# A planned attention and gate kernel: V made once per chunk and copied by DMA, a joint rsqrt chain, half the out transposes, output summed in DRAM

## The chip, the cores and the metric

One core of a Trainium2 chip runs the whole program. The metric is the device time of one execution in microseconds (us); of several executions the median is taken.

## The reference

```python
xn = _layernorm(x)                       # x: 1 x 2048 x 512, bf16
q = (xn @ wq)  -> 32 heads of 16         # wq: 512 x 512
k = xn @ wk ; v = xn @ wv                # one k and one v of 16 columns for all heads
p = softmax(q k^T * 16**-0.5)            # 32 heads x 2048 x 2048
s = concat_heads(p @ v) @ wo             # wo: 512 x 512
g = silu(silu(xn @ w1) @ w2)             # w1: 512 x 1792, w2: 1792 x 512
out = x + s * g
```

## The kernel before

The 2048 rows are 16 tiles of 128, in 4 chunks of 512 queries. A group g is one chunk of queries and four heads (half e of the eight-head block oi = g // 2); there are 32 groups. Each group has 64 slots: 32 blocks of 64 keys, times two head pairs i. One slot is one score unit: four matmuls 64x32 by 512 into one PSUM bank, and then an exponential of that bank (128x512). So there are 2048 units, 1240 of which ACT exponentiates and 808 DVE.

A unit's exponential is made in one of two ways:

- **On ACT**: an ACTIVATE Exp from PSUM into `pa_sb` (L1674), for one bank or for two banks at once.
- **On DVE**: one TENSOR_SCALAR from PSUM that writes the bits of a rough exponential into `db_sb` (L1042). Eight such slots make a batch. Three more copies of the batch with shifted bits are then made in `ds_sb`, by GpSimd's INT64_ADD on 64-bit words (one for each copy, L1225) or, near the end, by DVE (L1221). The four versions enter the sum with weights `SHIFT_W`.

The products with V (`do_pv`, L1303) go to one PSUM bank per group; V carries a column of weights so that the softmax's sum comes with it. `make_norm` then transposes the bank (L1320), takes a reciprocal (L1323), multiplies (L1325), and for each pair of groups transposes 128x512 into `on_sb` (L1335), from which the out projection reads. The MLP runs as jobs `h` and `z` (L705), the query projection as job `q`, the out projection as job `w` (L705, and L1514 and L591 for the last chunk).

TensorE is used as two lanes (rows and columns split, tiles of 64x32), fed from one queue: scores on lane 1, V products on lane 0, the halves of jobs on either.

**What sets the order.** The program is written by a planner (class `Planner`) that steps the five engines with a table of durations and latencies, picks the next piece for each, and writes down five instruction queues with the semaphore waits that they need. Each engine runs its queue in order. `Mix.draw` shakes the planner's thresholds once per stretch by the numbers in `SEEDS`, so the order is that of one drawn plan.

**The prologue.** Per chunk: BN_STATS of four tiles (L539), a chain of eight tiny DVE instructions for the inverse square root (L556 to L565, the tiles in sets `first`), the scaled tiles `xn_sb` (L568), transposes on TensorE (L607) and their copies `xnT_sb` (L618), then the jobs K (L633, copied by DVE in L651) and V. Job V (L670) makes each 64-key block twice, into PSUM rows 0 to 63 and 64 to 127:

```python
for r in (0, 64):
    h = pe.matmul(bank(b)[r:r + 64, t * DH:(t + 1) * DH],
                  lhsT=xnT_sb[:, dc, kb * 64:(kb + 1) * 64], rhs=wv_sb[:, dc, :],
                  start=(dc == 0), stop=(dc == NDC - 1), tile_position=(0, r), skip_group_check=True)
```

DVE then writes five weighted copies straight into `v_sb` (L679). GpSimd fills the weight columns of `v_sb` (L495), zeroes (L501, L497), and sends a shifted copy of the keys by DMA (L1349).

**The end of a row tile.** `final` makes two DVE passes of 128x512, the product with the gate (L814) and the sum with a reloaded x (`xr_sb`, L817), and stores `ob_sb` from SP (L809). The last four tiles take the path of the `tail` functions.

Of the kernel before, what the change touches and what calls it, by code (L numbers as in the profile page):

```python
# [22 lines left out]
SEEDS, STRETCH = [0, 0, 882634, 0, 348373, 328499, 78780, 554384, 89101, 903077, 320169, 0, 878569, 280070, 102111, 381856, 427096, 265022, 0, 740569, 0, 0, 0, 191854, 393933, 374197, 266972, 0, 665170, 0, 882882, 218695, 9227, 955074, 159633, 731624, 518155, 138034, 620799, 357599, 376984, 365473, 457970, 796664, 668429, 641664, 991272, 0, 0, 23990, 593814, 88565, 504692, 394759, 276845, 267858, 882770, 104810, 721623, 135503, 603776, 0, 337714, 100793, 638616, 0, 419715, 752789, 751312, 664693, 308960, 0, 762547, 276261, 218757, 897693, 0, 624478, 290921, 0, 713781, 335568, 417921, 100939, 814701, 0, 180062, 99721, 614963, 258262, 411291, 131548, 802432, 314922, 883804, 569039, 54637, 401726, 110613, 0, 983842, 914345, 0, 0, 0, 0, 0, 0, 0, 0], 6000.0  # L23
STG = lambda j, xn, ev: xn[4 * j - 1].op is not None
# [3 lines left out]
T_P64, DV_MIN, T_LIB = 1868.0, 40, 300.0  # L28
# [5 lines left out]
J_SLIP = 1.014  # L34
NEXT_OB, OB_SLACK = 8, 67.243
NORM_PRIO, T_DIV = 0, 264.0
A_OPEN = 1
T_MS, V_AT = 500.0, 9
T_TP, T_COLD, N_COLD = 56.0, 427.0, 11
# [16 lines left out]
NPA, NDB, NDS, NTM = 27, 3, 4, 4  # L56
MARGIN, MARGIN_END = 17, 20
# [5 lines left out]
ROOM = 1  # L63
# [4 lines left out]
MATE = 176.663  # L68
RH, EVR, SC_PRIO, PES = 0, (0, 2, 3), 0, (1, 0)
# [6 lines left out]
class Task:  # L76
    __slots__ = ("eng", "dur", "emit", "reads", "writes", "prio", "preds", "op", "on_place", "dma", "gate", "ports", "after", "ring", "first")

    def __init__(self, eng, dur, emit, reads=(), writes=(), prio=5, preds=(), on_place=None, dma=0, gate=None, ports=1):
        self.ports, self.after, self.ring = ports, None, None  # L80
# [9 lines left out]
    (DV, PE): 140.0, (DV, AC): 150.0, (DV, DV): 115.0, (DV, PO): 165.0, (DV, SP): 180.0,  # L90
# [5 lines left out]
class Planner:  # L96

    def __init__(self):
# [7 lines left out]
        self.held = None  # L106
# [3 lines left out]
        self.last2 = {DV: None, PO: None}  # L110

# [28 lines left out]
    def place(self, eng, dur, emit, reads, writes, dma=0, t0=None, ports=1, after=None):  # L140
# [23 lines left out]
        elif dma:  # L164
            start = max(t0 + 1400.0, self.dma_t if dma > 1 else 0.0)
# [14 lines left out]
    def tensor(self, mode, lane, dur, emit, reads, writes, t, after=None, n=8, held=None):  # L180
# [18 lines left out]
        if both or lane == 1:  # L199
            self.held = held  # L200
# [18 lines left out]
    def avail(self, task):  # L219
# [35 lines left out]
    def finalize(self, new_sem):  # L255
# [40 lines left out]
        for e in ENGINES:  # L296
            n = 0
            for op in self.order[e]:
# [53 lines left out]
def bass_recurrent_scan__grouped_kv_mqa__dense_activation_silu__prompt_kernel(  # L352
# [29 lines left out]
    with ExitStack() as es:  # L382
# [15 lines left out]
        v_sb = sb("v_sb", [P, K + 1, NKB, 2 * DH], BF16)  # L398
# [43 lines left out]
        xv = xf.rearrange("(t p) d -> p t d", p=P)  # L442

# [53 lines left out]
        pl.add(Task(PO, 1800.0, lambda g: g.memset(kt_sb[0:DH, 1, :], 0.0), [("xn", 3)], [("kt1", c) for c in range(NC)], 3,  # L497
                    gate=lambda: all(xn_task[t].op is not None for t in range(4)), ports=2))
# [36 lines left out]
        for j in range(4):  # L535
            for t in range(4 * j, 4 * j + 4):
                if t == 1:
# [3 lines left out]
                                  gate=(lambda j=j: STG(j, xn_task, evac_kt)) if j > 1 else  # L541
# [4 lines left out]
        first = (2, 2, 4, 4, 4)  # L546
# [75 lines left out]

        def xnT_keys(c):
            return [("xnT", t) for t in range(4 * c, 4 * c + 4)]

        def mk_K(c, ka, kb, bk=None):
# [13 lines left out]
            def consume(jb, op):  # L640
# [18 lines left out]
            job("K", c, 0.0, [(rnd(dc), ["wke"] + keys, max(64.0, n / 2.4 + 3.0)) for dc in range(NDC)], consume,  # L659
                bk=bk, gate=lambda: all(k in pl.lastw for k in keys))  # L660
# [1122 lines left out]
```

## Time and profile before

| | before |
|---|---|
| median of 3 runs | 658.52 us (658.26 to 658.54) |
| profiled execution, its span | 656.6 us (its own time is not given beside it; 1.9 us lie between the span and the median) |
| TensorE busy | 648.1 us (99%) |
| VectorE (DVE) busy | 639.3 us (97%) |
| ScalarE (ACT) busy | 640.4 us (98%) |
| GpSimd (POOL) busy | 571.0 us (87%) |
| granted TensorE clock | 1.00 in every stretch |
| HBM | 8.95 MB read, 2.10 MB written |

Busy is the union of an engine's records. A record of ACT or DVE begins before the one ahead of it has ended, so the sum of durations is above the busy time, and the step from one start to the next is what one instruction costs its engine when work is waiting. Matmuls overlap likewise, and a busy TensorE need not be a full one.

### The profile page before, as it was taken

The numbers are of one execution on the slowest core, as the hardware profiler recorded it, in microseconds if no ns is written. First come the engines' busy times: TensorE is split into PE (matmuls) and PEld (weight loads), VectorE is DVE, ScalarE is ACT, GpSimd is POOL, SyncE is SP. The second block draws the span as 40 slices with busy tenths as digits, with TensorE's granted clock in tenths as the row PEclk, the third lists the DMA queues.
The fourth block names the chain that finished last, engine by engine and source line by source line (L and its number), as shares of the span: only waits on it lengthen the run. The fifth ranks groups of instructions, "written<-read, shape, count | busy, mean of one in ns | idle before, by whom it ended". The sixth has DMA issues, their size and how long they took to land.

```text
span 656.6 us, 44475 instructions
## 1 busy us (share of the span) xinstructions
PE 648.1 (99%) x22180; PEld 330.7 (50%) x19436; DVE 639.3 (97%) x1170; ACT 640.4 (98%) x1128; POOL 571.0 (87%) x320
## 2 busy tenths in 40 slices
PE   8999999999999999999999999999999999999997
PEld 4445554544455554554555454444555555554444
DVE  8999999999999999999999999999999999999976
ACT  6889999999999999999999999999999999999995
POOL 4038899999998978999999878999999999889991
PEclk9999999999999999999999999999999999999999
DMA  6311111000011100000000010000000000100001
GB/s 177 129 48 42 42 28 29 10 4 10 5 35 28 35 28 4 10 4 6 9 4 12 20 36 26 4 5 9 5 10 4 10 21 20 35 11 5 4 4 34
DMA packets 13641, 15.92 MB, mean 24 GB/s; under 512 B 2320, under 2 KB 12816, under 8 KB 13456
## 3 DMA queue, kind: packets, MB, share of 16 engines
q1 hardware_dynamic: 12976, 12.36, 6.3%
q8 instruction: 162, 2.65, 1.7%
q0 software_dynamic: 192, 0.46, 0.2%
q10 hardware_dynamic: 288, 0.26, 0.1%
q14 instruction: 23, 0.19, 0.1%
HBM read 8.95 MB, written 2.10 MB: 17 GB/s over the span
## 4 chain that ended last, share of the span: by engine, by line
PE 84%; ACT 10%; DVE 3%; POOL 1%; DMA 0%; issue 0%
PE ps L967 28%; PE ps L1303 23%; PE ps L705 20%; PE ps L961 13%; ACT pa_sb L1674 9%; ACT t_sb L761 1%; DVE stats_sb L539 1%; DVE xn_sb L568 1%; PE ps L1514 1%; DVE xnT_sb L618 0%; DMA kt_sb<-kt_sb 0%; POOL qt_sb L501 0%; POOL kt_sb L497 0%; DVE v_sb L679 0%; DVE kt_sb L651 0%
## 5 line engine op out<-in xcount | busy, mean ns | idle before, releaser
L1674 ACT ACTIVATE pa_sb<-ps 128x512 bf16<-128x512 f32 (+1 forms) x1038 | 611.0, 771 | 4.1 <-PE ps L967 3.8
L1225 POOL INT64_ADD ds_sb<-db_sb x300 | 562.1, 1896 | 41.5 <-DVE db_sb L1042 31.9
L1042 DVE TENSOR_SCALAR db_sb<-ps 128x512 uint16<-128x512 f32 x808 | 499.9, 680 | 4.2 <-PE ps L961 2.0
L967 PE MATMUL ps<-qt_sb,kt_sb 64*32 64x512 bf16 x5448 | 470.6, 378 | 1.5 <-DVE v_sb L679 0.8
L1303 PE MATMUL ps<-ds_sb,v_sb 64*32 64x512 bf16 x4848 | 350.5, 377 | 0.0
L1303 PE MATMUL ps<-pa_sb,v_sb 64*32 64x512 bf16 x2480 | 269.9, 377 | 0.5 <-DVE v_sb L679 0.5
L961 PE MATMUL ps<-qt_sb,kt_sb 64*32 64x512 bf16 x2744 | 263.6, 375 | 0.0
L967 PEld LDWEIGHTS ps<-qt_sb,kt_sb 64*32 64x32 bf16 x5448 | 130.4, 89 | 162.8 <-ACT pa_sb L1674 70.6
L1303 PE MATMUL ps<-db_sb,v_sb 64*32 64x512 bf16 x1616 | 210.6, 377 | 0.0
L1303 PEld LDWEIGHTS ps<-ds_sb,v_sb 64*32 64x32 bf16 x4848 | 133.4, 91 | 43.5 <-issue 15.0
L705 PE MATMUL ps<-xnT_sb,w_sb 64*32 64x512 bf16 x1792 | 134.6, 377 | 0.0
L705 PE MATMUL ps<-w_sb,u_sb 64*32 64x512 bf16 x1792 | 133.5, 376 | 0.0
L1303 PEld LDWEIGHTS ps<-pa_sb,v_sb 64*32 64x32 bf16 x2480 | 91.4, 91 | 26.8 <-issue 7.9
L1303 PEld LDWEIGHTS ps<-db_sb,v_sb 64*32 64x32 bf16 x1616 | 66.5, 91 | 15.7 <-issue 5.3
L705 PEld LDWEIGHTS ps<-xnT_sb,w_sb 64*32 64x32 bf16 x1792 | 42.8, 91 | 24.9 <-issue 6.7
L705 PEld LDWEIGHTS ps<-w_sb,u_sb 64*32 64x32 bf16 x1792 | 44.4, 91 | 20.3 <-issue 6.2
L761 ACT ACTIVATE t_sb<-ps 128x512 bf16<-128x512 f32 x72 | 49.1, 682 | 0.0
L762 DVE SCALAR_TENSOR_TENSOR u_sb<-t_sb,ps 128x512 bf16<-128x512 bf16 x56 | 37.9, 677 | 1.0 <-ACT t_sb L761 1.0
L705 PE MATMUL ps<-xnT_sb,wq_sb 64*32 64x512 bf16 x480 | 37.1, 377 | 0.0
L705 PE MATMUL ps<-wo_sb,on_sb 64*32 64x512 bf16 x384 | 30.2, 377 | 0.0
L1320 DVE STREAM_TRANSPOSE ps<-ps 128x512 f32<-128x512 f32 (+1 forms) x33 | 23.2, 706 | 3.6 <-PE ps L1303 3.6
L1349 POOL DMA_DIRECT2D kt_sb<-kt_sb x4 | 2.3, 566 | 21.3 <-DVE rstd_sb L559 7.8
(78 smaller groups left out, 193.0 us busy)
## 6 DMA issues: line engine op xcount, KB each, us to landing
xr_sb<-in_A_x_dram SPq DMA_DIRECT2D x16, 128.0 KB, 2.4
out_dram<-ob_sb SPq DMA_DIRECT2D x16, 128.0 KB, 1.8
w_sb<-in_B_w_dram SPq DMA_DIRECT2D x1, 1792.0 KB, 7.3
w_sb<-in_B_w_dram SPq DMA_DIRECT2D x14, 128.0 KB, 2.1
ds_sb<-in_A_x_dram SPq DMA_DIRECT2D x3, 512.0 KB, 7.1
qt_sb<-qt_sb SPq DMA_DIRECT2D x16, 96.0 KB, 2.2
wq_sb<-in_A_wq_dram SPq DMA_DIRECT2D x1, 512.0 KB, 5.4
wo_sb<-in_A_wo_dram SPq DMA_DIRECT2D x4, 128.0 KB, 2.9
```

Of the source, the lines that this page charges most:

```text
L539: ts_ = pl.add(Task(DV, 593.0, lambda v, t=t: v.bn_stats(stats_sb[:, t, :], x_tile(t)), [xkey(t)], [("st", t)], 1 + j, gate=(lambda j=j: S ...
L568: xn_task[i] = pl.add(Task(DV, 323.0, lambda v, i=i: v.tensor_scalar(xn_sb[:, i % 4, :], x_tile(i), mv_sb[:, i, 0:1], rstd_sb[:, i:i + 1], ...
L705: h = pe.matmul(bank(b)[32 * j:32 * (j + 1), :], lhsT=lhs(k, rows, 32 * j, 32), rhs=rhs(k, rows), start=first, stop=last, tile_position=(r ...
L761: t1 = Task(AC, T_AF + 0.8333 * NQ, lambda a: a.activation(t_sb[:, k, :], bank(b), ACT.Tanh, scale=scale), [("ps", b)], [("t", k)], 0)
L762: t2 = Task(DV, T_P, lambda v: v.scalar_tensor_tensor(out=dst, in0=t_sb[:, k, :], scalar=1.0, in1=bank(b), op0=ALU.add, op1=ALU.mult), [(" ...
L961: h = pe.add_instruction(mybir.InstMatmult(name=pe.bass.get_next_instruction_name(), engine=mybir.EngineType.PE, ins=[pe.lower_ap(q), pe.l ...
L967: h = pe.matmul(to, lhsT=keys, rhs=q, start=True, stop=True, tile_position=(r0, 32 * j), skip_group_check=True)
L1042: bt.P[k] = pl.add(Task(DV, T_P, lambda v: v.tensor_scalar(db_sb[:, bt.b, k * NQ:(k + 1) * NQ], bank(b), 128.0 * LOG2E, 128.0 * (SHIFT_BET ...
L1225: whole["po"].append(pl.add(Task(PO, T_P64, lambda g: g.int64_add(ds_sb[:, s, :].bitcast(U64), db_sb[:, bt.b, :].bitcast(U64), words), rea ...
L1303: h = pe.matmul(bank(OB)[q:q + 32, :], lhsT=lhs[rows], rhs=rhs[rows], start=s0, stop=s1, tile_position=(64 * l, q), skip_group_check=True)
L1320: t1 = pl.add(Task(DV, (T_TR - 60.0) / parts + 60.0, lambda v, cols=cols: v.transpose(bank(OB)[:, cols], bank(OB)[:, cols]), [("ps", OB)], ...
L1674: op = pl.place(AC, 0.8333 * NQ * n + T_AF, lambda a: a.activation(pa3[:, k0:k1 + 1:max(1, k1 - k0), :], ps3[:, b0:b1 + 1:step, :], ACT.Ex ...
```

## The change

- **V** is made once per chunk, 128 keys at a time (`L718` now). DVE writes the five weighted copies into a new tile `vg_sb` of 128 keys a row block, and four DMAs from SP per chunk copy its two halves of 64 rows to both halves of `v_sb`, whose layout splits even and odd 64-key blocks. A V product waits for the two copies that it reads. GpSimd's weight columns go into `vg_sb` (eight times smaller fills).
- **rsqrt**: the tile sets are (2, 2, 8, 4) in place of (2, 2, 4, 4, 4); statistics of chunk 2 may start with those of chunk 1.
- **on_sb transposes** are done on pairs of bf16 as 32-bit words, 128x256, and the out projection reads every second column (`on_cols`).
- **Output**: for tiles 0 to 11, SP copies x from DRAM to the output in DRAM, DVE makes one pass (the product, into `ob_sb`), and GpSimd issues a DMA that adds `ob_sb` onto the output. Tiles 12 to 15 keep the old way.
- **Tail**: the out projection of the last chunk takes PSUM banks one by one (`tbk`) in place of waiting for seven free ones.
- `tmp_sb`, `xr_sb`, `fin_sb` are placed in memory of `xn_sb` and of `w1_sb`; `ds_sb` has five buffers in place of four. Two DVE passes may be joined into one of two banks (`both_passes`).
- Numbers of the planner and the whole of `SEEDS` are replaced. Several new branches are off by their numbers: `KU = 0` (K jobs stay as they were), `XBAR = 0`, `ZDMA = 0`, `S0A = 0`, and `PA`, `JA`, `FJ` of 900 to 9000.

The core of the diff:

```diff
-SEEDS, STRETCH = [0, 0, 882634, ...
+SEEDS, STRETCH = [0, 0, 0, 0, 0, 67544, ...
-STG = lambda j, xn, ev: xn[4 * j - 1].op is not None
+STG = {2: 3, 3: 11}
...
+KA = 0.0
+T_V = 250.0
+FIRST = (2, 2, 8, 4)
+KU, VG_PRIO, ROOM0 = 0, 0, 4
...
-NPA, NDB, NDS, NTM = 27, 3, 4, 4
-MARGIN, MARGIN_END = 17, 20
+NPA, NDB, NDS, NTM = 27, 3, 5, 4
+MARGIN, MARGIN_END = 24, 24
...
+TR32, XBAR, T_TURN = 1, 0, 500.0
+YIELD, W_LATE = 1, 0.0
+DK, PRO_PRIO, ZDMA = 12, 6, 0
...
-            pl.add(Task(PO, T_MS, lambda g, j=j: g.memset(v_sb[:, j, :, DH:], 1.0 if j == 0 else SHIFT_W[j - 1]),
+            pl.add(Task(PO, 150.0, lambda g, j=j: g.memset(vg_sb[:, j, :, DH:], 1.0 if j == 0 else SHIFT_W[j - 1]),
...
-                        for t in range(4 * k, 4 * k + 4):
-                            kb = 8 * c + t
+                        for t in range(2 * k, 2 * k + 2):
                             for dc in range(NDC):
-                                for r in (0, 64):
-                                    h = pe.matmul(bank(b)[r:r + 64, t * DH:(t + 1) * DH],
-                                                  lhsT=xnT_sb[:, dc, kb * 64:(kb + 1) * 64], rhs=wv_sb[:, dc, :],
+                                h = pe.matmul(bank(b)[:, t * DH:(t + 1) * DH], lhsT=xnT_sb[:, dc, (4 * c + t) * P:(4 * c + t + 1) * P],
...
-                t = Task(DV, 740.0, lambda v: v.tensor_tensor(
-                    v_sb[:, :, 8 * c:8 * c + 8, 0:DH],
+                t = Task(DV, 410.0, lambda v: v.tensor_tensor(
+                    vg_sb[:, :, :, 0:DH],
...
+                for h in range(2):
+                    for d in range(2):
+                        def emit(e, h=h, d=d):
+                            return e.dma_start(v_sb[64 * d:64 * d + 64, :, h, 4 * c:4 * c + 4, :], vg_sb[64 * h:64 * h + 64, :, :, :])
+                        last = pl.add(Task(SP, 100.0, emit, ["vg"] + [("Vw", j) for j in range(K + 1)], [("V", 2 * h + d, c)], -1, [last], dma=80 * 1024))
...
         def final(tt, b):
-            k = tt % 2
+            if tt < NT - 4:
+                t1 = Task(DV, T_P, lambda v: v.scalar_tensor_tensor(
+                    out=ob_sb[:, tt % 4, :], in0=bank(b), scalar=0.25, in1=tmp_sb[:, tt % NTM, :], op0=ALU.mult, op1=ALU.mult),
+                    [("ps", b), ("xn", tt % NTM)], [("ob", tt % 4)], 0, [tmp_task[tt], out_task.get(tt - 4)])
+                fin_task[tt] = t1
+                out_task[tt] = pl.add(Task(PO, T_SWDGE, lambda e: e.dma_start(ov[:, tt, :], ob_sb[:, tt % 4, :], accum_op=ALU.add),
+                                           [("ob", tt % 4)], [("out", tt)], 0, [t1, xr_task[tt]], dma=256 * 1024, on_place=outs.append))
+                return t1,
...
+            if tt < NT - 4:
+                xr_task[tt] = pl.add(Task(SP, 60.0, lambda e: e.dma_start(ov[:, tt, :], xv[:, tt, :]),
+                                          (), [("out", tt)], 2, [], dma=256 * 1024))
...
-        def v_lhs(j, kb):
-            return v_sb[:, j, kb, :]
+            return v_sb[:, j, kb % 2, kb // 2, :]
...
-                t2_task[oi] = pl.add(Task(DV, (T_TR - 60.0) / parts + 60.0, lambda v, cols=cols: v.transpose(
+                t2_task[oi] = pl.add(Task(DV, (T_TR - 60.0) / parts / (2 if TR32 else 1) + 60.0, lambda v, cols=cols: v.transpose(
+                    on_sb[:, oi % NON, cols].bitcast(FP32), otr_sb[:, oi % 2, cols].bitcast(FP32)) if TR32 else v.transpose(
...
-            if st["assigned"] == NG * SLOTS and st["expn"] == len(units) and len(pool_free) >= 7 and not tail["made"] and all(
-                    tt in tmp_task for tt in range(NT - 4, NT)):
+            if st["assigned"] == NG * SLOTS and not tail["made"] and all(tt in tmp_task for tt in range(NT - 4, NT)) and (
+                    not active and st["job"] == len(jobs) and NG - 1 in ob):
```

Three places show how the queues move. First DVE in the prologue, around the rsqrt chain of chunk 1 (`stats_sb`, `mv_sb`: statistics; `var_sb`, `rstd_sb`: the rsqrt chain; `vg_sb`, `v_sb`: V). Before:

```order
L556 TENSOR_SCALAR var_sb<-mv_sb 128x4
L559 TENSOR_SCALAR rstd_sb<-var_sb 128x4
L562 SCALAR_TENSOR_TENSOR var_sb<-rstd_sb 128x4
L564 TENSOR_TENSOR var_sb<-var_sb 128x4
L565 SCALAR_TENSOR_TENSOR rstd_sb<-var_sb,rstd_sb 128x4
L562 SCALAR_TENSOR_TENSOR var_sb<-rstd_sb 128x4
L564 TENSOR_TENSOR var_sb<-var_sb 128x4
L565 SCALAR_TENSOR_TENSOR rstd_sb<-var_sb,rstd_sb 128x4
L679 TENSOR_TENSOR v_sb<-ps,wj_sb 128x5x8x16
L568 TENSOR_SCALAR xn_sb<-ds_sb,mv_sb,rstd_sb 128x512 x4
L539 BN_STATS stats_sb<-ds_sb 128x6
L618 COPY xnT_sb<-ps 128x4x256 x2
```

Now:

```order
L581 BN_AGGR mv_sb<-stats_sb 128x2 x2
L594 TENSOR_SCALAR var_sb<-mv_sb 128x8
L597 TENSOR_SCALAR rstd_sb<-var_sb 128x8
L600 SCALAR_TENSOR_TENSOR var_sb<-rstd_sb 128x8
L602 TENSOR_TENSOR var_sb<-var_sb 128x8
L603 SCALAR_TENSOR_TENSOR rstd_sb<-var_sb,rstd_sb 128x8
L600 SCALAR_TENSOR_TENSOR var_sb<-rstd_sb 128x8
L602 TENSOR_TENSOR var_sb<-var_sb 128x8
L603 SCALAR_TENSOR_TENSOR rstd_sb<-var_sb,rstd_sb 128x8
L606 TENSOR_SCALAR xn_sb<-ds_sb,mv_sb,rstd_sb 128x512 x4
L656 COPY xnT_sb<-ps 128x4x256 x2
L606 TENSOR_SCALAR xn_sb<-ds_sb,mv_sb,rstd_sb 128x512 x4
```

One chain now serves chunks 1 and 2 (the statistics of chunk 2 stand ahead of it), V of chunk 0 has moved ahead of the chain, and the scaled tiles of chunk 2 follow the copies of chunk 1 directly.

Then TensorE from the first scores to the first V products (`ps<-qt_sb,kt_sb`: scores, x4 is one unit; `ps<-wv_sb,xnT_sb`: job V; `ps<-ident,xn_sb`: transposes; `ps<-pa_sb,v_sb`: V products). Before:

```order
L967 MATMUL ps<-qt_sb,kt_sb 32x512 x32
L961 MATMUL ps<-qt_sb,kt_sb 32x512 x4
L670 MATMUL ps<-wv_sb,xnT_sb 64x16 x64
L967 MATMUL ps<-qt_sb,kt_sb 32x512 x20
L1303 MATMUL ps<-pa_sb,v_sb 32x512 x4
```

Now:

```order
L1036 MATMUL ps<-qt_sb,kt_sb 32x512 x32
L1030 MATMUL ps<-qt_sb,kt_sb 32x512 x4
L718 MATMUL ps<-wv_sb,xnT_sb 128x16 x16
L1036 MATMUL ps<-qt_sb,kt_sb 32x512 x32
L1030 MATMUL ps<-qt_sb,kt_sb 32x512 x4
L1036 MATMUL ps<-qt_sb,kt_sb 32x512 x4
L645 MATMUL ps<-ident,xn_sb 128x128 x16
L1383 MATMUL ps<-pa_sb,v_sb 32x512 x4
```

Nineteen units and the transposes of chunk 1 now stand ahead of the first V product, against fourteen units before.

Last the end of TensorE's queue (`ps<-wo_sb,on_sb`: the out projection of the last chunk). Before:

```order
L1303 MATMUL ps<-ds_sb,v_sb 32x512 x4
L1514 MATMUL ps<-wo_sb,on_sb 32x512 x4
L1303 MATMUL ps<-pa_sb,v_sb 32x512 x4
L1514 MATMUL ps<-wo_sb,on_sb 32x512 x72
L591 MATMUL ps<-wo_sb,on_sb 32x512 x16
```

Now:

```order
L1383 MATMUL ps<-pa_sb,v_sb 32x512 x4
L1615 MATMUL ps<-wo_sb,on_sb 32x512 x32
L1383 MATMUL ps<-pa_sb,v_sb 32x512 x4
L1615 MATMUL ps<-wo_sb,on_sb 32x512 x28
L1383 MATMUL ps<-pa_sb,v_sb 32x512 x4
L1615 MATMUL ps<-wo_sb,on_sb 32x512 x24
L1655 MATMUL ps<-w_sb,ident 128x512 x2
L629 MATMUL ps<-wo_sb,on_sb 32x512 x16
```

Twenty-four matmuls of the projection's first part are left behind the last V product, against seventy-two before.

More of the change, by code (lines that the diff above doesn't have):

```diff
@@ L309, in finalize @@
                     op.sem, op.val = sems[e], n
+        for e in ENGINES:
+            for op in self.order[e]:
+                if op.ring is not None:
+                    op.val = rings[op.ring][1]
     def run_engine(self, e, handle):
@@ L658, in mk_K @@
             keys = [("xnT", t) for t in range(ka, kb)]
-            job("K", c, 0.0, [(rnd(dc), ["wke"] + keys, max(64.0, n / 2.4 + 3.0)) for dc in range(NDC)], consume,
-                bk=bk, gate=lambda: all(k in pl.lastw for k in keys))
+            jb = job("K", c, 0.0, [(rnd(dc), ["wke"] + keys, max(64.0, n / 2.4 + 3.0)) for dc in range(NDC)], consume,
+                     bk=bk, gate=lambda: all(k in pl.lastw for k in keys))
+            if KU and n == NQ:
+                product(jb, lambda k, rows, a, n: wke_sb[rows, k, a:a + n], lambda k, rows: xnT_sb[rows, k, ka * P:kb * P],
+                        lambda k: ["wke"] + keys)
         def mk_V(c):
@@ L1305, in emit @@
                 return h
-            pl.tensor("U", 0, MM, emit, sorted(reads, key=str), [("ps", OB)], t, n=4 * len(mm))
+            last = ob_last.get(g)
+            ob_last[g] = pl.tensor("U", lane, MM, emit, sorted(reads, key=str), [("ps", OB)], t, n=4 * len(mm),
+                                   after=last if last is not None and last.lane != lane else None)
             make_shifts()
@@ L1473, in make_tail @@
             c = NC - 1
-            tb.extend([b for _, b in bank_times()])
             for r in range(4):
@@ L1693, in generic_step @@
             now, soon = pl.best(e, t)
+            if now is not None and now[1].slot is not None and both_passes(max(t, now[2]), now[1]):
+                return True
             if now is not None:
```

301 lines of the change are left out of this document (208 added, 93 removed).

## The prediction

> **What bounds the kernel now.** I read the page's busy shares first, then the busy time by stretch, with cuts at ACT's first exponential (11.51), at two of its starts in the prologue and at its last exponential's end (646.90).
>
> ```profile
> span 656.6 us, 44475 instructions
> PE 648.1 (99%) x22180; PEld 330.7 (50%) x19436; DVE 639.3 (97%) x1170; ACT 640.4 (98%) x1128; POOL 571.0 (87%) x320
> ```
>
> ```profile
> core 0: us, PE busy (x) PEld busy (x) DVE busy (x) ACT busy (x) POOL busy (x), PEclk, DMA share, GB/s
> 11.51:26.45 14.94, 13.43 (x332) 6.28 (x292) 13.24 (x43) 14.22 (x24) 3.58 (x5) 1.00 0.44 148
> 26.45:38.83 12.38, 11.55 (x334) 6.05 (x312) 10.57 (x29) 9.59 (x15) 0.82 (x2) 1.00 0.06 15
> 38.83:646.90 608.07, 607.95 (x21292) 311.05 (x18600) 600.88 (x1030) 607.97 (x1071) 562.31 (x301) 1.00 0.06 17
> 646.90:656.60 9.70, 5.66 (x128) 2.82 (x108) 4.62 (x14) 2.64 (x6) 0.00 (x0) 1.00 0.17 57
> ```
>
> From 38.83 to 646.90 ACT has a record open in 607.97 of 608.07 us, so on the face of it ACT sets the time and the rest hides behind it. But records overlap. What one instruction costs ACT is the step between starts, and the count of its groups then gives a floor.
>
> ```profile
> L1674 ACT ACTIVATE pa_sb<-ps 128x512 bf16<-128x512 f32 x836 | 446.2, 694 | 2.6 <-PE ps L967 2.4
> L1674 ACT ACTIVATE pa_sb<-ps 128x1024 bf16<-128x1024 f32 x202 | 213.7, 1090 | 1.5 <-PE ps L967 1.4
> L761 ACT ACTIVATE t_sb<-ps 128x512 bf16<-128x512 f32 x72 | 49.1, 682 | 0.0
> ```
>
> ```profile
> 440.09 0.73 ACT L761 ACTIVATE t_sb<-ps 128x512 bf16<-128x512 f32 x1
> 440.57 5.58 ACT L1674 ACTIVATE pa_sb<-ps 128x512 bf16<-128x512 f32 x10
> ```
>
> ```profile
> 630.58 2.85 ACT L1674 ACTIVATE pa_sb<-ps 128x1024 bf16<-128x1024 f32 x3
> 633.29 0.63 ACT L761 ACTIVATE t_sb<-ps 128x512 bf16<-128x512 f32 x1
> ```
>
> A 512-wide ACTIVATE steps by 440.57 - 440.09 = 0.48 us, a 1024-wide one by (633.29 - 630.58) / 3 = 0.90. The floor is 836 x 0.48 + 202 x 0.90 + 72 x 0.48 = 617.7 us. From 11.51 to 646.90 are 635.4, so ACT waits 17.7 us: 0.72 + 2.79 + 0.10 = 3.6 visible, nearly all in the prologue, and 14.1 hidden under overlapping records. The span is 11.5 ahead of the first exponential, 617.7 of work, 17.7 of waits and 9.7 of tail: 656.6.
>
> Who keeps ACT waiting is read from the waits: TensorE's one queue stops at scores for want of a free PSUM bank, and everything behind stops with it.
>
> ```profile
> PEld ps L967 <- ACT pa_sb L1674: 70.6, 292, 0.5
> PEld ps L967 <- DVE db_sb L1042: 35.7, 165, 0.4
> POOL ds_sb L1225 <- DVE db_sb L1042: 31.9, 25, 5.7
> PEld ps L1303 <- POOL ds_sb L1225: 2.3, 8, 0.4
> ```
>
> **Part by part: ACT's work.** The new queues hold 828 single, 206 double exponentials and 72 tanh: 397.4 + 185.4 + 34.6 = 617.4. The split of units between ACT and DVE (1240 to 808) is unchanged, so the floor falls by only 0.3 us. Whatever the rest removes counts only where it shortens ACT's waits or the ends.
>
> **DVE.**
>
> ```profile
> L817 DVE TENSOR_TENSOR ob_sb<-ps,xr_sb 128x512 bf16<-128x512 f32 x12 | 8.1, 677 | 0.0
> L1335 DVE STREAM_TRANSPOSE on_sb<-otr_sb 128x512 bf16<-128x512 bf16 x15 | 10.5, 702 | 0.0
> L1335 DVE STREAM_TRANSPOSE on_sb<-otr_sb 128x256 bf16<-128x256 bf16 x2 | 0.8, 418 | 0.0
> L1221 DVE TENSOR_SCALAR ds_sb<-db_sb 128x4096 uint16<-128x4096 uint16 x3 | 3.5, 1222 | 0.0
> ```
>
> ```profile
> 310.53 4.86 DVE L1042 TENSOR_SCALAR db_sb<-ps 128x512 uint16<-128x512 f32 x8
> ```
>
> A full pass from PSUM steps by (4.86 - 0.68) / 7 = 0.60. Twelve sum passes go (7.2), fifteen transposes shrink by 0.702 - 0.418 = 0.28 each (4.3, with the two halves of the last), V and the joined chain give 2.9 (next part); three more shift passes cost 3 x 1.17 = 3.5. Only eight passes are joined, in four pairs: nothing worth a term. Net 10.9 us of 639.3. It is off the chain except through the banks that DVE frees late: 35.7 of 106.3 us of such stops. A third of the hidden 14.1 is 4.7, and I take half of it back: **-2.5**. The bounds are -14 (all hidden waits gone) and +7 (half as much again, since the order is drawn anew).
>
> **The prologue.**
>
> ```profile
> 13.01 0.17 DVE L556 TENSOR_SCALAR var_sb<-mv_sb 128x4 f32<-128x4 f32 x1
> ...
> 14.40 0.17 DVE L565 SCALAR_TENSOR_TENSOR rstd_sb<-var_sb,rstd_sb 128x4 f32<-128x4 f32 x1
> 14.92 0.82 DVE L679 TENSOR_TENSOR v_sb<-ps,wj_sb 128x640 bf16<-128x640 f32 x1 [0.36 <-PE ps L670]
> 16.50 0.41 DVE L568 TENSOR_SCALAR xn_sb<-ds_sb,mv_sb,rstd_sb 128x512 bf16<-128x512 bf16 x1 [0.76 <-POOL kt_sb L497]
> ```
>
> ```profile
> 39.20 3.07 DVE L1042 TENSOR_SCALAR db_sb<-ps 128x512 uint16<-128x512 f32 x5
> ```
>
> ```profile
> 18.18 0.62 PE L607 MATMUL ps<-ident,xn_sb 128*128 128x128 bf16 x8
> 29.86 1.18 PE L670 MATMUL ps<-wv_sb,xnT_sb 128*64 128x16 bf16 x64
> ```
>
> Eight links step by (14.40 - 13.01) / 7 = 0.20, so one chain less saves 1.6 us of DVE. V's weighted copies shrink from 640 to 320 columns; by the 0.28 that 256 columns cost above, 0.33 each, 1.3 in all. The 0.76 behind GpSimd's zeroing goes if that comes earlier. DVE then reaches its first exponential pass some 3.7 us before 39.20. Chunk 1 itself comes later, for four statistics (4 x 0.60) go ahead of its chain, but chunk 0 holds 32 units, 32 x 0.48 = 15 us of work for ACT after 11.51, which covers it. On TensorE, V's 64 matmuls take 1.18 per chunk, 16 ns apart. The sixteen new ones have twice the columns of weights: between 2 x 16 = 32 ns and the (0.62 - 0.22) / 7 = 57 of the transposes, 0.5 to 0.9 and a drain of 0.2; I take 0.9, 1.1 us saved in all. ACT's visible idle in the prologue (3.5) sits behind such work, and I take 2.5 back: **-2.5**, bounds -3.5 and +2.
>
> The Trainium skill speaks against this step: in "TensorE: Matmul & The Clock Gate", section "LDWEIGHTS (loading the stationary operand)", a load costs its columns divided by 1.2 ns, 107 ns for 128, so an estimate of 1.7 us per chunk in place of 0.9. The sum would then end 3 us later. Its 53 ns for 64 columns does not fit the 16 ns of the row above, so I do not follow it.
>
> **V's copies.** Sixteen DMAs are new, on SP, four per chunk.
>
> ```profile
> qt_sb<-qt_sb SPq DMA_DIRECT2D x16, 96.0 KB, 2.2
> w_sb<-in_B_w_dram SPq DMA_DIRECT2D x1, 1792.0 KB, 7.3
> kt_sb<-kt_sb POOLq DMA_DIRECT2D x4, 112.0 KB, 3.5
> ```
>
> ```profile
> 3.23 1.73 SPq L445 DMA_DIRECT2D ds_sb<-in_A_x_dram  x3
> ```
>
> An issue takes 1.73 / 3 = 0.58 of SP, a landing 2.2 to 3.5: V is usable 4 x 0.58 + 2.2 = 4.5 us (up to 5.8) after DVE's write, where it was usable at once. For chunk 0 the cover is nineteen units (9 us of ACT) and the transposes of chunk 1; for later chunks the exponentials already waiting in 27 `pa_sb` buffers, less what the 1792 KB load of 7.3 us holds up. If the cover fails TensorE stands at the first V product with all scores behind it: 0 to 2 us per chunk. I take **+0.5** in all, bounds 0 and 6. The four warm-up matmuls more end at about the first transposes: 0 to 0.2.
>
> **GpSimd.**
>
> ```profile
> L1225 POOL INT64_ADD ds_sb<-db_sb x300 | 562.1, 1896 | 41.5 <-DVE db_sb L1042 31.9 <-PE ps L1303 8.0 <-PE ps L961 1.0
> L1349 POOL DMA_DIRECT2D kt_sb<-kt_sb x4 | 2.3, 566 | 21.3 <-DVE rstd_sb L559 7.8 <-DVE kt_sb L651 7.4 <-DVE mv_sb L543 6.1
> ```
>
> Three adds less (-5.7), twelve issues of 0.57 more (+6.8), each waiting in the queue for a DVE pass and for SP's copy. The 41.5 us of idle cover it: **0**, and the second rival if not. The SP stores and x reloads that go had no waiter.
>
> **The tail.**
>
> ```profile
> 647.63 2.85 PE L1514 MATMUL ps<-wo_sb,on_sb 64*32 64x512 bf16 x68
> 647.95 0.80 DVE L1320 STREAM_TRANSPOSE ps<-ps 128x256 f32<-128x256 f32 x2 [1.47 <-PE ps L1303]
> 649.26 0.76 DVE L1335 STREAM_TRANSPOSE on_sb<-otr_sb 128x256 bf16<-128x256 bf16 x2
> 650.42 1.05 PE L591 MATMUL ps<-wo_sb,on_sb 128*32 128x512 bf16 x16
> ```
>
> Now 24 in place of 72 projection matmuls stand behind the last V product, so TensorE is free nearly 2 us earlier. But L591 also needs the transposes, which end at 650.02: only 0.3 to 0.4 comes of it, plus about 0.2 for the halved transposes. **-0.5**, bounds -1 and +1.
>
> **Sum.** 656.6 - 0.3 - 2.5 - 2.5 + 0.5 - 0.5 = 651.3 of span, and 1.9 to the median of 658.52, taken as unchanged: **653.2 us**.
>
> **The rivals.** *The hidden waits nearly go.* Two thirds of the 14.1 (9.4 in place of 2.5) give 653.2 - 6.9 = 646.3. For it: three engines get lighter. Against: 70.6 of the bank stops end with ACT itself.
>
> *GpSimd falls behind (slower).* Each of the twelve issues stands in one queue with the adds, and waits there for DVE. A wait of 1.0 with the issue costs 1.57, 18.8 in all. The idle of 0.14 per add takes eleven adds to make that up; if the tiles of one chunk come closer than this, half of it stops TensorE at V products of shifted copies: 653.2 + 9.4 = 662.6. It decides once the wait at an issue is above about 0.5 us. Against it: such stops are 2.3 us now.
>
> *V's copies come late.* 1.3 us at each of four chunks takes the prologue's gain: 653.2 + 2.5 + 5.2 - 3 hidden behind buffers = 657.9, no change.
>
> *The new order is worse.* Hidden waits up by half, 7, in place of 2.5 down: 662.7.
>
> The change's own words on the k projections do nothing: that branch is off, and the rows of job K are the same.
>
> **The numbers.** Forecast 0.57 (its own range 649.5 to 657), hidden waits 0.16, late V 0.09, GpSimd 0.09, new order 0.09. Faster by over 0.2% (about what a measurement here can tell from no change) are the first two, 0.73; within it 0.09; slower 0.18. The range of 8 in 10 takes in most of the better rival and reaches towards the slower ones: 645.5 to 661.
>
> **What would show it.** Right: ACT's visible idle before its steady stretch near 1 us, that stretch starting some 3 us earlier, its floor unchanged and waits near 12; the tail near 9.2. Wrong: V products waiting on DMA in the prologue; GpSimd idle at its issues with TensorE waiting on `ds_sb`; or hidden waits above 14.

## The result: slower by half a per cent, and the loss lies in the first 50 us

| | before | after |
|---|---|---|
| median of 4 runs each | 658.39 us | 661.81 us (660.63 to 662.38) |
| ratio | | 1.0048 (95%: 1.0034 to 1.0062) |
| span of the profiled execution | 656.6 us | 660.2 us |

The forecast was 653.2 us, a gain. The page of the kernel after has the same load on TensorE, less on VectorE, and a longer span:

```profile
span 660.2 us, 44477 instructions
PE 648.1 (98%) x21992; PEld 339.1 (51%) x19600; DVE 633.4 (96%) x1149; ACT 641.3 (97%) x1124; POOL 573.0 (87%) x329
```

The groups (count, then busy us and mean ns) show ACT's work as counted from the queues, and the cheaper transposes:

```profile
L1805 ACT ACTIVATE pa_sb<-ps 128x512 bf16<-128x512 f32 x828 | 440.9, 689 | 6.3 <-PE ps L1036 6.1
L1805 ACT ACTIVATE pa_sb<-ps 128x1024 bf16<-128x1024 f32 x206 | 215.1, 1089 | 1.3 <-PE ps L1030 0.7 <-PE ps L1036 0.5
L1425 DVE STREAM_TRANSPOSE on_sb<-otr_sb 128x256 f32<-128x256 f32 x15 | 6.5, 436 | 0.1
```

TensorE's stops at scores (total, times, longest) still end with ACT twice as often as with VectorE, 71.5 and 31.8 us where it was 70.6 and 35.7:

```profile
PEld ps L1036 <- ACT pa_sb L1805: 71.5, 298, 0.9
PEld ps L1036 <- DVE db_sb L1114: 31.8, 147, 0.4
```

To see where ACT loses time, take at a time t the sum of t and the own steps of all ACT instructions that have not started (0.479 us for 512 columns, 0.905 for 1024, near the commonest steps in the trace). It is the end that ACT would reach if it never waited again; what it grows by between two times is what ACT lost there. On this scale the kernel before stands at 636.35 at 50 us, the one after at 639.99. Worked out from ACT's starts in each trace, with the tail beside them (the first column holds ACT's work in the tail too, so a row adds up to some 2.2 us more than its span; the differences between the rows stand):

| profiled execution | ACT's work and start | lost 12 to 26 us | lost 26 to 50 | lost 50 to 645 | tail after the last exponential |
|---|---|---|---|---|---|
| before | 631.40 | 1.31 | 3.64 | 12.90 | 9.6 |
| after | 631.24 | 3.89 | 4.86 | 13.61 | 8.8 |

Of 3.6 us more span, 3.8 were lost ahead of 50 us, 0.7 after it; the tail and ACT's work gave 1.0 back. The place is seen in the timeline of the kernel after (start, duration, engine, line; in brackets the idle time before and what ended it):

```profile
15.26 0.47 DVE L726 TENSOR_TENSOR vg_sb<-ps,wj_sb 128x320 bf16<-128x320 f32 x1
15.76 2.70 SPq L735 DMA_DIRECT2D v_sb<-vg_sb  x4
18.33 1.27 PE L645 MATMUL ps<-ident,xn_sb 128*128 128x128 bf16 x16
21.63 0.62 PE L1383 MATMUL ps<-pa_sb,v_sb 64*32 64x512 bf16 x4 [2.03 <-DMA v_sb<-vg_sb]
22.32 0.60 ACT L1805 ACTIVATE pa_sb<-ps 128x512 bf16<-128x512 f32 x1 [1.73 <-PE ps L1036]
23.88 1.32 PE L680 MATMUL ps<-xnT_sb,wke_sb 128*32 128x512 bf16 x16
25.26 0.75 DVE L698 TENSOR_SCALAR kt_sb<-ps,part_sb 128x512 bf16<-128x512 f32 x1 [3.04 <-PE ps L680]
```

In the kernel before, where VectorE writes `v_sb` itself by 15.74 (the row at 14.92 in the prediction), the first V product follows 0.34 us later:

```profile
16.08 0.40 PE L1303 MATMUL ps<-pa_sb,v_sb 64*32 64x512 bf16 x4
```

Now VectorE has written V of chunk 0 at 15.73. SP sends the four copies one after another, and the first V product starts at 21.63, 5.9 us later. It is next in TensorE's queue when the transposes of chunk 1 end at 19.60, so TensorE stands for 2.03 us, and behind it stand the scores that ACT needs and job K of chunk 1. The chain of waits of the kernel after now names DMA v_sb<-vg_sb with 1% of the span.

The stand is followed by slow matmuls. In the stretches (length, busy time of PE, PEld, DVE, ACT and POOL, then the granted clock) the clock falls to half:

```profile
18.50:21.60 3.10, 1.07 (x16) 0.72 (x13) 3.03 (x9) 2.10 (x4) 0.00 (x0) 0.92 0.78 181
21.60:24.00 2.40, 2.37 (x36) 0.77 (x36) 0.62 (x2) 1.01 (x2) 0.00 (x0) 0.50 1.01 391
24.00:26.40 2.40, 2.40 (x58) 1.00 (x51) 1.14 (x3) 1.40 (x3) 0.07 (x1) 0.90 0.51 206
```

Chunks 2 and 3 have the same stand in small:

```profile
32.67 0.48 DVE L726 TENSOR_TENSOR vg_sb<-ps,wj_sb 128x320 bf16<-128x320 f32 x1
37.49 0.40 PE L1383 MATMUL ps<-pa_sb,v_sb 64*32 64x512 bf16 x4 [1.24 <-issue]
40.40 0.49 DVE L726 TENSOR_TENSOR vg_sb<-ps,wj_sb 128x320 bf16<-128x320 f32 x1
45.03 0.09 PEld L1383 LDWEIGHTS ps<-pa_sb,v_sb 64*32 64x32 bf16 x1 [0.51 <-DMA v_sb<-vg_sb]
```

The profile puts the 1.24 us down to "issue", nothing that it shows. But the instruction at 37.49 is the first in TensorE's queue that reads V of chunk 2, 4.3 us after VectorE wrote it, and in the trace the second copy of chunk 2 lands at 37.40. An experiment below decides it.

### The profile page after: what moved, and what is told of

It is laid out like the page before. It is cut to its first block, busy times and chain, and to the rows that moved or that the text cites. A ratio compares the mean times of both kernels' runs of the same rounds, so it can differ in the third digit from the quotient of the medians.

```text
span 660.2 us, 44477 instructions
## 1 busy us (share of the span) xinstructions
PE 648.1 (98%) x21992; PEld 339.1 (51%) x19600; DVE 633.4 (96%) x1149; ACT 641.3 (97%) x1124; POOL 573.0 (87%) x329
## 3 DMA queue, kind: packets, MB, share of 16 engines
q0 software_dynamic: 1920, 2.03, 2.4%
## 4 chain that ended last, share of the span: by engine, by line
PE 94%; DVE 2%; ACT 1%; DMA 1%; issue 0%; SPq 0%
PE ps L1036 31%; PE ps L1383 30%; PE ps L758 20%; PE ps L1030 13%; ACT pa_sb L1805 1%; DVE stats_sb L577 1%; DMA v_sb<-vg_sb 1%; PE ps L1615 1%; PE ps L680 0%; PE ps L645 0%; SPq L735 0%; DVE w_sb L853 0%; PE ps L718 0%; DVE mv_sb L581 0%; DVE xnT_sb L656 0%
## 5 line engine op out<-in xcount | busy, mean ns | idle before, releaser
L1036 PE MATMUL ps<-qt_sb,kt_sb 64*32 64x512 bf16 x5800 | 486.1, 379 | 1.5 <-ACT pa_sb L1805 0.8
L1383 PE MATMUL ps<-ds_sb,v_sb 64*32 64x512 bf16 x4848 | 356.4, 376 | 0.0
L1383 PE MATMUL ps<-pa_sb,v_sb 64*32 64x512 bf16 x2480 | 256.8, 379 | 3.8 <-DMA v_sb<-vg_sb 2.0
L1030 PE MATMUL ps<-qt_sb,kt_sb 64*32 64x512 bf16 x2392 | 231.1, 376 | 0.0
L1036 PEld LDWEIGHTS ps<-qt_sb,kt_sb 64*32 64x32 bf16 x5800 | 139.6, 89 | 160.2 <-ACT pa_sb L1805 71.5
L1383 PE MATMUL ps<-db_sb,v_sb 64*32 64x512 bf16 x1616 | 181.9, 377 | 0.0
L1383 PEld LDWEIGHTS ps<-ds_sb,v_sb 64*32 64x32 bf16 x4848 | 137.9, 91 | 41.3 <-issue 14.8
L758 PE MATMUL ps<-xnT_sb,w_sb 64*32 64x512 bf16 x1792 | 138.8, 377 | 0.0
L1383 PEld LDWEIGHTS ps<-pa_sb,v_sb 64*32 64x32 bf16 x2480 | 86.3, 91 | 29.4 <-issue 10.3
L1383 PEld LDWEIGHTS ps<-db_sb,v_sb 64*32 64x32 bf16 x1616 | 58.6, 91 | 15.4 <-issue 5.0
```

Source lines behind the costliest of these rows:

```text
L758: h = pe.matmul(bank(b)[32 * j:32 * (j + 1), :], lhsT=lhs(k, rows, 32 * j, 32), rhs=rhs(k, rows), start=first, stop=last, tile_position=(r ...
L1030: h = pe.add_instruction(mybir.InstMatmult(name=pe.bass.get_next_instruction_name(), engine=mybir.EngineType.PE, ins=[pe.lower_ap(q), pe.l ...
L1036: h = pe.matmul(to, lhsT=keys, rhs=q, start=True, stop=True, tile_position=(r0, 32 * j), skip_group_check=True)
L1383: h = pe.matmul(bank(OB)[q:q + 32, :], lhsT=lhs[rows], rhs=rhs[rows], start=s0, stop=s1, tile_position=(64 * l, q), skip_group_check=True)
```

## The experiments

The theory: V by four DMAs in a row lets the first V product of chunks 0, 2 and 3 start 5.9, 4.3 and 4.1 us after VectorE's write, the plan puts the first V products into TensorE's queue too early for that, and everything behind them waits. Rivals: the new order as such; the joined rsqrt chain; and for the missing gains, that VectorE was never what ACT waits for. In most kernels the five queues are kept as planned, and only the named instructions change. Each comparison is with the kernel before, run in turn with it. The profiled executions give the losses of ACT.

**1. V straight into `v_sb`.** Changed against the kernel after, order kept:

```diff
-matmul(bank[:, t * DH:...], lhsT=xnT_sb[:, dc, 128 rows], rhs=wv_sb)            # 16 per chunk, and 4 DMAs per chunk on SP
+for r in (0, 64): matmul(bank[r:r + 64, ...], lhsT=xnT_sb[:, dc, 64 rows], ...)  # as before; VectorE writes v_sb, no DMA
```

> The changed kernel with its order of every queue kept, but V made as in the kernel before: TensorE writes both halves (64 matmuls per chunk), VectorE writes v_sb itself, SP's sixteen copies are gone. Theory (V's copies at chunk 0 hold TensorE, and after the stand its matmuls run slower): the first V product moves from 21.6 us to about 17, ACT's waits ahead of 26 us fall from 3.9 us to 1 or less, and the time from 661.8 to about 658.3 (657.5 to 659.5). Rival, the new order as such: the waits only move to a later place of the prologue, 661 to 662.5. Rival, the joined rsqrt chain brings chunk 1 late: job K of chunk 1 stays near 23.9 us, 660.5 or more.

Measured: 658.48 us (12 runs, 657.36 to 661.06), ratio 0.9996 (0.9985 to 1.0008). ACT loses 1.30 us from 12 to 26 us and 3.81 to 50, the values of the kernel before, and no clock below 1.00 is left in the stretches. The profiled execution, 657.36, is the fastest of the twelve. So V's copies, with the readers where the plan put them, carry the whole loss, to within the 1 us that the interval leaves. TensorE spends more on V again, and the time does not show it. The order as such and the joined chain are out as causes of the loss: both are still in.

**2 and 3. Copies on two queues, and copies behind spare ones.** Chunk 0 only:

```diff
-SP: copy 0, copy 1, copy 2, copy 3
+SP: copy 0, copy 1      GpSimd: copy 2, copy 3                       # v_two_queues
+SP: spare x 4, copy 0, copy 1, copy 2, copy 3                        # v_twice
```

> The changed kernel, but the third and fourth copy of chunk 0 are issued on GpSimd's queue, which is idle there, in place of SP's. Theory (serial issues and landing set when V is there): the last copy is out up to 1.35 us earlier, unless GpSimd's own issue and landing take longer; first V product at 20.3 to 21 us and 660.4 to 661.3. If the landing is what counts and not the issue, no change. Rivals of order or chain: 661.8, no change.

> The changed kernel, but four spare copies of the same size stand ahead of chunk 0's four on SP (they go to places that are written anew later). Theory: V comes 2.7 us later (4 issues of 0.68), the first V product at 24.3 us, and the time is 661.8 + 2.7 = 664.5 (664 to 665.5), as ACT has nothing in hand there. Rivals, order or chain: the copies are covered, 661.8 to 662.3.

The first got 663.92 us (ratio 1.0072, 1.0056 to 1.0089), the second 667.07 (1.0120, 1.0104 to 1.0135). In the first, the copies went out by 17.53 us in place of 18.46, but landed no earlier (the timeline, and the DMA issues with KB each and us to landing):

```profile
15.86 1.36 SPq L735 DMA_DIRECT2D v_sb<-vg_sb  x2
16.15 1.38 POOL L735 DMA_DIRECT2D v_sb<-vg_sb  x2 [2.52 <-DVE mv_sb L581]
21.68 0.40 PE L1383 MATMUL ps<-pa_sb,v_sb 64*32 64x512 bf16 x4 [1.97 <-DMA v_sb<-vg_sb]
38.23 0.40 PE L1383 MATMUL ps<-pa_sb,v_sb 64*32 64x512 bf16 x4 [1.76 <-issue]
```

```profile
v_sb<-vg_sb POOLq DMA_DIRECT2D x2, 80.0 KB, 3.8
v_sb<-vg_sb SPq DMA_DIRECT2D x14, 80.0 KB, 3.4
```

My expectation missed: the time of the landing, not of the issue, set this one, and the later stands grew, which I can't explain by the two moved issues. In the second the first V product started at 23.83, 2.2 us later, the stand became 3.75 us and the time rose by some 5 us, more than the 2.7 expected: ACT lost 5.83 us by 26 us, and the clock was 0.55 from 24 to 26.4. By 50 us, though, ACT had lost 10.42 us against 8.75, 1.7 us for the 2.2 us of lateness. The rest of the 5 us came behind 50 us, and this run does not explain it.

**4. The planner is told what a copy costs.**

```diff
-Task(SP, 100.0, emit, ["vg"] ..., dma=80 * 1024)
+Task(SP, 675.0, emit, ["vg"] ..., dma=230 * 1024)
```

> The changed kernel with two numbers of its planner set to what the trace shows: 675 ns for an issue of V's copies in place of 100, and a landing of the last about 5.8 us after VectorE's write. The whole order is drawn anew. Theory: the first V products move behind chunk 1's work in TensorE's queue, ACT's waits ahead of 26 us fall from 3.9 us to 1 or less, and at 50 us the kernel is 2 to 3.5 us ahead of the changed one; 658 to 660 if the rest of the order is as good. Rival, a new order costs by itself: 661 or more, with the loss behind 50 us.

661.73 us, ratio 1.0043 (1.0031 to 1.0055). Up to 50 us the theory holds in kind: the stand is 0.57 us, the clock stays 1.00, ACT loses 4.37 us in place of 8.75 and stands at 635.69, a gain of 4.3 us where 2 to 3.5 were expected (ahead of 26 us it still loses 1.7, not 1 or less). But from 50 to 645 it loses 17.25 in place of 13.61. The whole order is drawn anew, and the new one has given back what the prologue won.

**5 and 6. Is it VectorE or TensorE that ACT waits for in the steady stretch?** On top of 1, order kept; parts of the results are left out:

```diff
-v.tensor_scalar(db_sb[..., 512 columns], bank(b), ...)
+v.tensor_scalar(db_sb[..., 256 columns], bank(b)[:, 0:256], ...)        # v_direct_dve_half
-pe.matmul(bank(b)[...], lhsT, rhs)
+pe.matmul(bank(b)[..., 0:256], lhsT, rhs[:, 0:256])   # jobs h and z    # v_direct_pe_half
```

> v_direct with its order kept, but VectorE's exponential passes from PSUM cover 256 of their 512 columns once each buffer place has been written in full (the other columns hold old values), some 200 us less work for VectorE. The prediction's step (a third of ACT's hidden waits are VectorE's, and go when it gets lighter): TensorE's stops for VectorE (29.7 us) nearly vanish, ACT loses 5 to 7 us less between 50 and 645 us than the 12.8 of v_direct, 651.5 to 653.5. Rival (ACT's waits come from the ring of ACT and TensorE alone): those stops vanish too, others take their place, 657.5 to 658.5.

> v_direct with its order kept, but the matmuls of the h and z products cover 256 of 512 columns (the rest of the bank holds old values), some 49 us less of TensorE's time. If TensorE, busy 99% of the span, is what makes ACT wait in the steady stretch: most of the 12.8 us lost there go, 647 to 651. If the steps of 0.491 us between ACT's exponentials are mostly its own: 656.5 to 658.5.

Measured 659.31 us (1.0002, 0.9989 to 1.0014) and 658.88 (0.9997, 0.9981 to 1.0013): nothing, for 151 us less of VectorE in the one, and for matmuls of the h and z products of 272 ns in place of 377 in the other. The waits (in total, times, longest) of v_direct, of v_direct_dve_half behind its busy times, and of v_direct_pe_half:

```profile
PEld ps L1039 <- ACT pa_sb L1808: 73.3, 307, 0.8
PEld ps L1039 <- DVE db_sb L1117: 29.7, 136, 0.4
```

```profile
PE 648.4 (99%) x22184; PEld 349.3 (53%) x19792; DVE 482.2 (73%) x1149; ACT 640.8 (98%) x1124; POOL 574.9 (88%) x329
PEld ps L1039 <- ACT pa_sb L1811: 91.2, 364, 0.8
PEld ps L1039 <- DVE db_sb L1120: 1.3, 6, 0.3
```

```profile
PEld ps L1040 <- ACT pa_sb L1809: 100.6, 384, 0.8
```

With the lighter VectorE, TensorE's stops for VectorE are gone, and stops for ACT stand in their place; with the lighter products too, TensorE stops longer for ACT. ACT loses 13.58 and 13.33 us from 50 to 645, against 12.76: making either neighbour lighter does not shorten what ACT loses.

ACT's starts in the trace of v_direct tell what the loss is made of. From 50 to 645 us most steps behind a 512-wide ACTIVATE are alike: the middle half of the 858 take 0.477 us. But 98 exceed 0.479 by 0.03 us or more, and these hold all of the 9.8 us that the 858 take above 0.479 each. With the 1024-wide ones, 115 of 1047 starts are late by that much, 11.3 us in all, and each of the 115 comes 0.022 or 0.023 us after an update by TensorE of the semaphore that ACT waits for. In v_direct_dve_half it is 111, 100 of them the same instructions of the queue. So most of the loss is waits of ACT for TensorE, at certain places of the order, hidden under overlapping records; it is not that each of ACT's steps is a little longer. Why TensorE is late at these places is not shown.

**7. Another order of the same work.** On top of 1, with the same prologue:

```diff
-SEEDS = [8 entries, then 101 more]
+SEEDS = [8 entries, then zeros]
```

> v_direct with the same prologue, but the table of draws is set to zero from its ninth entry, so the order of the queues is another one from 48 us on, of the same work. If an order picked by its table is worth something by itself: ACT loses 2 to 5 us more between 50 and 645 us, 660.5 to 663.5. If orders of the same work are alike: 658 to 659.

662.16 us, 1.0045 (1.0029 to 1.0062). Two things: 163 double exponentials in place of 206, 43 x (2 x 0.479 - 0.905) = 2.3 us more work for ACT, and 15.21 us lost from 50 to 645 in place of 12.76. An order has a price, and the one drawn for the kernel after is, by experiment 1, no worse than that of before (12.76 and 12.90).

**8. The old rsqrt chain in kernel 4.**

```diff
-FIRST = (2, 2, 8, 4)
+FIRST = (2, 2, 4, 4, 4)      # and the old gates
```

> v_told with the rsqrt chain as in the kernel before (2, 2, 4, 4, 4 tiles, the old gates), all else the same; the order is drawn anew. Only the stretch up to 50 us is to be compared. If the joined chain gives VectorE's 1.6 us to the prologue: ACT is 1 to 2 us further behind at 50 us than in v_told. If it costs by bringing chunk 1 late: 0.5 to 1 us ahead. The time itself, 660 to 665, depends on the order drawn.

664.40 us (1.0073, 1.0052 to 1.0095). At 50 us ACT has lost 6.29 us in place of 4.37. That is the size expected if the joined chain helps. But the redrawn order also made TensorE stand 0.95 us for the w1 load and 1.25 us behind an MLP pass of VectorE, so the run does not show it.

**9. Only TensorE's order.** Copies, planner and plan as in the kernel after; five groups of V products move:

```diff
-PE: T T | V-product, score, 2 V-products, score, V-product, score, V-product | K of chunk 1
+PE: T T | 3 scores | K of chunk 1 | 5 V-products
```

> The changed kernel with its copies, planner and order, but the five groups of V products that stand ahead of job K of chunk 1 in TensorE's queue are put behind it (the scores and K go first). Theory (nothing is wrong with the copies' time; what costs is that scores and chunk 1 stand behind a V product that comes too early in the queue): TensorE does not stand for DMA, its granted clock stays at 1.00, kt of chunk 1 is written near 22 us in place of 25.3, ACT loses 3 to 4 us less by 50 us, and the time is 658 to 659. Rival (the copies cost by their traffic, or the loss is the order as such): 660.5 or more.

662.37 us, 1.0047 (1.0033 to 1.0061): the time did not move. The prologue did what was expected up to 26 us: no stand, clock 1.00, kt of chunk 1 written from 22.22 in place of 25.26, 1.31 us lost. Then the next stands came:

```profile
35.00 0.40 PE L1383 MATMUL ps<-pa_sb,v_sb 64*32 64x512 bf16 x4 [1.25 <-issue]
43.38 0.39 PE L1383 MATMUL ps<-pa_sb,v_sb 64*32 64x512 bf16 x1 [0.90 <-DMA v_sb<-vg_sb]
```

With them ACT loses 5.43 us from 26 to 50, so by 50 us it is 2.0 ahead of the kernel after, not 3 to 4; and it loses 17.67 after that. The profiled execution is the slowest of the five (664.27), so the last figure is an extreme one.

**10. V straight for chunk 0 alone, copies for the others.** As 1, for c == 0 only.

> The changed kernel with its order, but chunk 0 alone gets V the old way (both halves on TensorE, VectorE writes v_sb in two instructions), chunks 1 to 3 keep the copies. Theory (only chunk 0's copies are late; ACT's buffers cover the others): as v_direct, 658.3 to 659. Rival of the prediction (1.3 us at each chunk): 660 to 661.5. If the stand of 1.24 us at 36 us in the changed kernel comes with the copies of chunk 2, it is still there and the time is 659.3 to 660.

659.79 us (10 runs), 1.0008 (0.9997 to 1.0019). Two stands for v_sb are left, 0.51 and 0.50 us. So chunk 0 is most of the loss. Against experiment 1 the later copies cost 0.8 us by the ratios (1.0008 and 0.9996), and the two intervals overlap.

**11. All V products that come too early are moved.**

```diff
 v_moved
+PE: first V-product of chunk 2 behind K of chunk 3; first two of chunk 3 behind two more scores
```

> v_moved, and besides the first V product of chunk 2 goes behind job K of chunk 3, and the first two groups of chunk 3's behind two more groups of scores; copies and the rest of the order as in the changed kernel. Theory (the stand of 1.25 us at chunk 2, which the trace puts down to issue, is the wait for chunk 2's copies, as is the 0.5 at chunk 3): both go, TensorE has no stand over 0.4 us up to 50 us, ACT is 1.5 to 1.9 us ahead of v_moved there, and the time is 1.3 to 1.9 us below v_moved's 662.4. If that stand is a fetch of instructions it stays where it is, and the time is that of v_moved.

658.95 us (12 runs, 657.60 to 661.97), 1.0006 (0.9993 to 1.0018). No idle time of 0.4 us or more for DMA or issue is left on TensorE from 18 to 50 us:

```profile
18.50:21.60 3.10, 3.06 (x50) 1.30 (x47) 3.03 (x8) 3.10 (x6) 0.00 (x0) 1.00 0.79 192
21.60:24.00 2.40, 2.40 (x68) 1.15 (x56) 2.06 (x5) 1.40 (x3) 0.55 (x1) 1.00 1.01 394
35.00:50.00 15.00, 14.88 (x438) 6.85 (x386) 13.45 (x23) 13.27 (x25) 9.68 (x6) 1.00 0.30 78
```

ACT loses 4.92 us by 50 us, as before the change (4.94). The stand put down to issue is gone with the move of one V product, so it was the wait for chunk 2's copies. Against experiment 9 the time fell by 2.7 us by the ratios, where 1.3 to 1.9 were expected; 1.8 of it is there at 50 us. With all sixteen copies in place, eight groups in another place of one queue take the ratio from 1.0048 to 1.0006, some 2.8 us.

**12. Both.** Kernel 10 with the V products of chunks 2 and 3 moved as in 11.

> v_direct_first (chunk 0's V written straight, copies for chunks 1 to 3), with the first V products of chunks 2 and 3 put back in TensorE's queue as in v_moved_all. Theory: its two stands of 0.51 and 0.50 us for the copies go, ACT is about 1 us ahead of v_direct_first at 50 us (635.0 in place of 636.0 on the same scale), and the time is 658.3 to 659, level with the kernel before or up to 1 us below it. If the steady stretch gives it back, 659.8.

657.49 us (12 runs, 656.24 to 659.81), ratio 0.9984 (0.9972 to 0.9996): the only one whose interval lies below 1, by a little. ACT loses 4.31 us by 50 us and 13.89 to 645, and the tail is 8.4.

## The prediction, step by step

*ACT's floor, -0.3.* Right: 828 and 206 exponentials as counted, and the start of the scale 0.2 lower.

*VectorE lighter, -2.5.* Wrong, and the step that failed first. I called 14.1 us between ACT's records "hidden waits" and gave a third of them to VectorE, since a third of TensorE's stops end with it. Waits they are for the most part: in experiment 1, 11.3 of the 12.76 us lost are late starts of ACT behind TensorE. But how often TensorE's stops end with VectorE does not say what ACT gets back. Experiment 5 takes 151 us off VectorE, the stops which ended with it are replaced by stops which end with ACT, and ACT loses 13.58 us in place of 12.76. VectorE did get lighter in the kernel after, by 5.9 us of busy time where I had counted 10.9, and no time came of it: ACT lost 0.7 us more from 50 to 645, not 2.5 less.

*The prologue, -2.5.* Mis-sized. Without late copies it is 4.3 to 5.1 us of ACT's loss up to 50 us (experiments 12, 11 and 1) against 4.94, a gain of 0.6 at best. I had put ACT's idle behind VectorE; in the rows of experiment 11 TensorE is the fuller engine there, 2.40 of 2.40 and 14.88 of 15.00 us against 2.06 and 13.45. That it sets ACT's waits in the prologue is read from these shares and was not tested by itself. My price for V on TensorE was even too high: 0.56 us per chunk, not 0.9.

```profile
25.91 0.56 PE L718 MATMUL ps<-wv_sb,xnT_sb 128*128 128x16 bf16 x16
```

The rule of the Trainium skill that I set aside ("TensorE: Matmul & The Clock Gate", section "LDWEIGHTS (loading the stationary operand)", 107 ns for 128 columns, an estimate of 1.7 us) does not fit this row either.

*V's copies, +0.5.* This step turned the sign. The latency was right: 4.5 to 5.8 us stood there, and the last copies of the four chunks landed 5.9, 4.9, 5.0 and 4.9 us after VectorE's write. The cover was counted wrongly. I set nineteen units, 9 us of ACT, against it. They are there, but from 11.56 on, and they end near 20.4: when VectorE writes V at 15.73, nine of them are used up and only some 5 us of cover are left, less the time from a score to its exponential. What I listed as further cover, the transposes of chunk 1, lies ahead of the V product only; the scores and K behind it are not cover, they are what waits. Its cost, for which I had 0.5, is the 3.6 us between the kernel after and experiment 1 up to 50 us (8.75 - 5.11). The first of my signs of being wrong, V products that wait on DMA in the prologue, is the one that came.

*The rival "V's copies come late"* had the mechanism, chance 0.09. Its price was 1.3 us at each of four chunks, 3 of them hidden. Measured stands are 2.03, none, 1.24 and 0.5, and the half clock after the first on top.

*GpSimd, 0.* Right: its DMA issues waited 2.1 us in all, and the stretch behind 50 us lost 12.76 in experiment 1 with all of them in.

```profile
POOL out_dram L871 <- DVE ob_sb L867: 2.1, 3, 1.0
```

*The tail, -0.5.* Right in kind, 0.9 to 1.2 in size: ACT's wait ahead of its last three passes, 3.88 us before (the first line), is 2.66 (the second).

```profile
650.87 1.57 ACT L798 ACTIVATE xn_sb<-ps 128x512 bf16<-128x512 f32 x3 [3.88 <-PE ps L591]
654.08 1.57 ACT L851 ACTIVATE w_sb<-ps 128x512 bf16<-128x512 f32 x3 [2.66 <-PE ps L629]
```

*The new order.* As an explanation of this result it is out. Experiments 4 and 7 show that it could have been one: their orders lost 3.6 and 2.5 us more from 50 to 645 us.

*The sum.* The forecast was 651.3 us of span, and 660.2 were measured. Of the 8.9 us between them some 3.1 are V's copies (3.6 for 0.5), 2.7 the prologue without them (5.11 against 4.94, where 2.5 was to be gained) and 3.2 the steady stretch (0.7 lost for 2.5 gained); the tail gave 0.4 more than forecast.

**What stays open.** With one and the same order, ACT's loss from 50 to 645 us ran from 12.76 to 17.67 in the profiled executions, and executions of one kernel lie up to 4.8 us apart (v_direct_pe_half). What makes TensorE late for ACT in that stretch is open. Why experiment 9 shows nothing of its 2 us at 50 us in the time is not settled, nor why the copies of one chunk take so unlike times to land, 2.3, 2.3, 4.1 and 3.8 us for chunk 0 of the kernel after. The load of w1, which SP issues behind them at 18.50, is not needed for it: in experiment 3 it goes out at 22.20, and the third and fourth of the eight copies still take 4.0 and 3.6.

## What to carry to other kernels

Cover has a beginning as well as a length: count what is left of it when the new wait starts, not what there was in all. In an in-order queue the question is not how long a DMA takes but what stands behind the first instruction that reads it; if that can go ahead, moving a few instructions in the queue was worth some 2.8 us here. And before giving time back for a lighter engine, ask which stop would end last without it: a stop that ends with one engine may end with another at nearly the same moment, as 151 us less of VectorE showed here.

## What the hardware did that I had not expected

- TensorE's granted clock fell to half after a short stand. With 2.03 us of stand it was 0.50 over the next 2.4 us, with 3.75 us 0.55, with 1.97 us 0.73 and then 0.55, with 0.57 or none 1.00. The length of the stand alone does not tell it: one of 1.76 us, ahead of 38.23 in experiment 2, left the clock at 1.00. The Trainium skill ("TensorE: Matmul & The Clock Gate", section "What's actually happening") has the half clock follow an idle window of about 3.4 us; the run shows it after a stand of 2.03 us in a stretch where TensorE was busy for 1.07 of 3.10.
- A wait for a DMA can appear as "issue" in the profile: 1.24 us here, shown by the landing at 37.40 and by moving the instruction.
- An 80 KB copy from SBUF to SBUF took 0.68 us of SP to issue (2.70 / 4) and 3.0 us to land, the median of sixteen that took 2.2 to 4.1. Two issued from GpSimd's queue took 2.8 and 4.8.
